# A gated delta-rule attention with a softplus MLP on one core: eight PSUM banks in one ring, and every item in a new order

## The chip, the core and the metric

The kernel runs on one core of a Trainium2 chip. The metric is the device time of one execution in microseconds (us), lower is better. The core has a matrix engine (PE; its weight loads are shown as PEld), VectorE (DVE), ScalarE (ACT), GpSimd (POOL) and SyncE (SP). Each works through its own list of instructions in order. DMAs are issued from the lists of SP, ACT and POOL and move data between memory (HBM) and SBUF. PE writes its results to PSUM, which is cut here into eight tiles of 128 x 512 floats, called banks in this text; DVE and ACT read them out.

## What is computed

Four batches and eight heads (32 in all), 768 time steps, head width 48. For each head a 48 x 48 state is carried through time:

```python
B, H, S, D = q.shape                       # 4, 8, 768, 48
k_n = k / (np.linalg.norm(k, axis=-1, keepdims=True) + 1e-06)
state = np.zeros((B, H, D, D)); y = np.zeros_like(q)
for t in range(S):
    readout = einsum('bhd,bhde->bhe', q[:, :, t], state)
    y[:, :, t] = g[:, :, t] * readout
    v_old = einsum('bhde,bhd->bhe', state, k_n[:, :, t])
    state += beta[:, :, t, None, None] * outer(k_n[:, :, t], v[:, :, t] - v_old)
```

The result, as 3072 tokens of 384 features, goes through a two-layer MLP, with `w_in` 384 x 2048 and `w_out` 2048 x 384:

```python
x = y.transpose(0, 2, 1, 3).reshape(3072, 384)
h = x @ w_in
out = softplus(h) @ w_out
```

## The kernel before

**Tiling.** Time is cut into 12 chunks of 64 steps. Within a chunk the recurrence is turned into small matrix products: the strictly triangular system that each chunk's keys make is inverted, and the state passes from chunk to chunk. Two batches sit side by side on the 128 partitions, so a 64-row product fills a quarter of PE and four of them run at a time. The chunks' systems are inverted in six pairs (`GROUPS`).

**Items.** The code first records the work as items (`Program.add`), each with the engines that may do it, what it depends on, and the buffers it uses. By name, in the order in which one chunk runs through them:

- `load` (L302, L305): q, k, v, g of a chunk, two DMAs of 192 KB each, from SP.
- `ksq`, `red`, `sqrt` or `pow`, `eps` (L351 to L383): the norm of k. `cast` or `kmul` (L209, L211, L406): q and k to fp16. `trs` (L422, L454): their transposes on PE. `kev`, `qev`: eviction of these from PSUM into `kqt`.
- `gram` (L516; for chunks 0 and 1 split into `gramk` and `gramq`, with `gramd`, L540, for the diagonal blocks): the products of keys with keys and queries. `kkc`, `kd`: evictions into `kk`, `dn`. `mask` (L498): the masked part into `mt`.
- `ln`, `pick`, `prep`, `step` (L597 to L671): the forward substitution of 16 x 16 blocks for a pair of chunks, 15 steps on DVE or POOL. `ca`, `cb` (L686, L688): the result as fp16 into `ta` and `tw`. `st` (L714): DVE transposes `ta` into `dn` and `tw` into `tb` and `td`. `tx`: a copy of half of `tb` to the other partitions.
- `xmm` (L744), `xs` (L753), `tmm` (L768), `td2`, `zmm` (L789), `z`: the inverse is put together from its blocks.
- The chain through the state: `ks` and `qs` (L826), `w` (L866), `umm` (L880), `u1`, `zu` (L893), `u2`, `smm` (L910), `s` (L924), `ymm` (L936), `y` (L950), `ytr` (L963), `xt`. Each hop is a product on PE and an eviction by DVE or ACT.
- The MLP: `g1` (L989), `soft` (L1001, the softplus on ACT), `g2` (L1016), `o` (eviction into `osb`), `store` (L1035). 96 `g1` and 96 `g2`; a `g2` is four of the 16 products that a sum in PSUM needs, so four `g2` share a bank. `wload` (L330) brings the weights, from POOL.
- `fill` (L1046): four products of the identity that nobody reads. 40 are recorded, and the order uses as many as it names.

Copies and evictions go through one helper, so all have the line L209 (on ACT), L211 or L213.

**Order.** Nothing is scheduled at run time. The string `_ORDER` names every item once with its engine letter (P, D, A, G for POOL, S), and `emit` issues them in that order: each engine gets its own items in the order of the string. A buffer is taken from its ring when the first item that uses it is emitted, and goes to the ring's end when the last one is. An item waits on the chip for what it depends on and for the last reader of the buffer's earlier content.

**PSUM.** The banks are three rings: five (`d`) for all products of the attention, two (`h`) for `g1` and fills, one (`o`) for the sums of `g2`:

```python
p_d = ring("d", 5, [P, 512], F32, psum)
p_h = ring("h", 2, [P, 512], F32, psum)
p_o = ring("o", 1, [P, 512], F32, psum)
```

**PE's two modes.** Products of 64 rows or fewer (gram, xmm, tmm, zmm, and the chain) use parts of the array, and transposes, g1, g2 and fills use all of it. The text calls a change from the one kind to the other in PE's list a border.

## Time and profile before

| | |
|---|---|
| runs | 242.34, 242.52, 244.88 us; median 242.52 |
| profiled execution, first to last instruction | 241.5 us |
| its own time beyond the span | not given; the median lies 1.0 us above the span |
| instructions | 11396, of them 5020 products on PE |
| data read / written by DMA | 25.26 MB / 4.72 MB, 124 GB/s over the span |
| first `g1` / last `g2` ends | 40.5 us / 237.6 us |

How to read the views that follow. The page's first part gives each engine's busy time, share of the span and number of instructions; a row of digits gives tenths in 40 equal slices, and PEclk the clock that PE was granted. In the timeline a row is start, duration, engine, line, operation, out<-in with sizes, a count, and in brackets how long the engine was idle before it and what ended that. PE's products are pipelined: a row's duration holds the time until the last one has drained, so the cost of a group is the distance from its start to the next group's start. The view by stage gives busy time and instructions of each engine between two moments.

### The profile page before, as it was taken

Reading aid. Unit: us, or ns where it says so; the run is one execution under the profiler, and the core shown is the slowest. Engines: PE = TensorE matmul, PEld = TensorE weight load, DVE = VectorE, ACT = ScalarE, POOL = GpSimd, SP = SyncE. Lnnn points to the kernel's source line nnn. Section 1 sums busy time; section 2 is a strip of 40 time slices with the busy share of each in tenths; the row PEclk is TensorE's granted clock in tenths of the full one; section 3 lists DMA queues with packets and bytes.
Section 4 is the critical chain, followed back from the end, with each engine's and each line's share of the span. In section 5 each row is a group of like instructions: output and inputs, shape, how many; then the busy total and the mean of one; then the engine's idle time right before and its main releaser. Section 6 shows DMA issues by size and latency. Waiting matters only on the chain.

```text
span 241.5 us, 11396 instructions
## 1 busy us (share of the span) xinstructions
PE 219.4 (91%) x5020; PEld 135.6 (56%) x5020; DVE 161.7 (67%) x368; ACT 152.8 (63%) x292; POOL 113.7 (47%) x197
## 2 busy tenths in 40 slices
PE   7645877879988999999999999999999999999983
PEld 2423455646764664556655566655565555677751
DVE  2768699888897889987899757896496310623000
ACT  5767576764982778876895767757363674143540
POOL 8740393875779778989597482016620000000000
PEclk9985599999999999999999999999999999999999
DMA  6999989999999399961889514962302311303112
GB/s 102 182 245 137 167 135 190 176 173 180 180 217 167 57 177 164 162 113 35 150 153 184 97 30 94 160 122 52 69 21 52 68 34 25 64 19 81 35 33 65
DMA packets 86833, 27.57 MB, mean 114 GB/s; under 512 B 77048, under 2 KB 86776, under 8 KB 86784
## 3 DMA queue, kind: packets, MB, share of 16 engines
q1 hardware_dynamic: 80624, 20.83, 52.6%
q0 software_dynamic: 3840, 3.17, 8.5%
q10 hardware_dynamic: 2320, 2.85, 5.2%
q8 instruction: 39, 0.64, 1.2%
q14 instruction: 10, 0.08, 0.1%
HBM read 25.26 MB, written 4.72 MB: 124 GB/s over the span
## 4 chain that ended last, share of the span: by engine, by line
PE 75%; DMA 7%; DVE 6%; SPq 4%; issue 3%; ACT 2%; POOL 1%; DVEq 0%; ACTq 0%; POOLq 0%
PE o L1016 27%; PE h L989 26%; DMA w_in<-in_moe_w_in_dram 4%; PE d L826 3%; SPq L305 3%; PE d L936 3%; PE d L516 2%; DMA f<-in_q_dram 2%; PE d L422 2%; PE d L963 2%; PE d L454 2%; PE d L880 2%; PE d L910 2%; PE d L893 2%; PE d L768 1%
## 5 line engine op out<-in xcount | busy, mean ns | idle before, releaser
L1016 PE MATMUL o<-w_out,ga 128*128 128x384 f16 x384 | 77.7, 327 | 0.7 <-ACT osb L209 0.6
L1001 ACT ACTIVATE ga<-h 128x512 f16<-128x512 f32 x96 | 56.5, 599 | 29.8 <-PE h L989 25.9
L989 PE MATMUL h<-xt,w_in 128*128 128x512 f16 (+1 forms) x384 | 74.0, 327 | 0.5 <-DMA w_in<-in_moe_w_in_dram 0.3
L989 PEld LDWEIGHTS <-w_in 128*128 128x128 f16 x384 | 34.5, 98 | 21.2 <-DMA w_in<-in_moe_w_in_dram 0.8
L1016 PEld LDWEIGHTS <-ga 128*128 128x128 f16 x384 | 33.7, 98 | 21.8 <-issue 0.8
L664 POOL TENSOR_TENSOR tmp<-nn,tt 128x78 f32<-128x78 f32 (+7 forms) x53 | 19.2, 362 | 16.1 <-DVE tt L671 13.0
L373 POOL TENSOR_TENSOR nv<-nv,half_c 128x16 f32<-128x16 f32 x8 | 23.5, 2940 | 6.6 <-DVE nv L362 6.5
L671 POOL TENSOR_TENSOR tt<-tt,tmp 128x78 f32<-128x78 f32 (+7 forms) x53 | 20.4, 385 | 4.2
L498 DVE TENSOR_TENSOR mt<-d,mask 128x256 f16<-128x256 f32 x48 | 18.2, 413 | 4.5 <-PE d L516 3.5
L209 ACT ACTIVATE kqt<-d 128x1024 f16<-128x1024 f16 (+1 forms) x18 | 18.0, 1000 | 4.8 <-PE d L454 3.6
L211 DVE CAST u<-d 128x384 f16<-128x384 f32 x20 | 10.9, 554 | 14.3 <-PE d L880 7.9
L209 ACT ACTIVATE u<-d 128x384 f16<-128x384 f32 x28 | 13.0, 490 | 11.8 <-PE d L880 5.4
L1046 PE MATMUL h<-ident 128*128 128x512 f16 x52 | 18.1, 493 | 1.7 <-DVE ident L197 1.7
L209 ACT ACTIVATE kk<-d 128x256 f16<-128x256 f32 x37 | 13.4, 386 | 6.3 <-PE d L516 5.4
L209 ACT ACTIVATE osb<-o 128x384 f32<-128x384 f32 x19 | 9.3, 492 | 9.4 <-PE o L1016 9.3
L454 PE MATMUL d<-ident,qn 128*128 128x128 f16 x96 | 8.5, 243 | 6.7 <-ACT qn L209 5.9
L950 DVE TENSOR_TENSOR yg<-d,f 128x384 f16<-128x384 f32 x24 | 12.3, 551 | 2.9 <-PE d L936 2.8
L924 DVE TENSOR_TENSOR s<-s,d 128x384 f16<-128x384 f16 x20 | 10.4, 542 | 5.7 <-PE d L910 4.3
L644 POOL TENSOR_TENSOR nn<-ln,beta_l 128x256 f32<-128x256 f16 x8 | 6.1, 780 | 14.2 <-DVE ln L627 14.2
L209 ACT ACTIVATE xt<-d 128x768 f16<-128x768 f16 x10 | 8.1, 813 | 7.0 <-PE d L963 7.0
L866 DVE TENSOR_TENSOR w<-f,d 128x384 f16<-128x384 f32 x22 | 11.3, 545 | 1.4 <-ACT xt L209 0.7
L362 DVE TENSOR_REDUCE nv<-f 128x16 f32<-128x768 f32 x12 | 11.3, 942 | 1.0 <-ACT f L351 1.0
(117 smaller groups left out, 346.7 us busy)
## 6 DMA issues: line engine op xcount, KB each, us to landing
f<-in_k_dram SPq DMA_DIRECT2D x24, 192.0 KB, 5.7
f<-in_q_dram SPq DMA_DIRECT2D x24, 192.0 KB, 5.6
f<-in_v_dram SPq DMA_DIRECT2D x24, 192.0 KB, 5.3
f<-in_g_dram SPq DMA_DIRECT2D x24, 192.0 KB, 5.3
out_dram<-osb ACTq DMA_DIRECT2D x29, 96.0 KB, 2.7
out_dram<-osb SPq DMA_DIRECT2D x19, 96.0 KB, 2.8
w_in<-in_moe_w_in_dram POOLq DMA_DIRECT2D x4, 384.0 KB, 7.9
w_out<-in_moe_w_out_dram POOLq DMA_DIRECT2D x4, 384.0 KB, 8.4
```

Of the source, the lines that this page charges most:

```text
L209: nc.scalar.activation(o, x, AF.Copy, scale=float(sign))
L362: lambda en: nc.vector.tensor_reduce(nvs().rearrange("p (a h) -> p a h", a=2), ksq.ap, mybir.AxisListType.X, ALU.add),
L373: nc.gpsimd.tensor_tensor(nvs(), nvs(), half_c[:, :NU], ALU.pow)
L454: nc.tensor.transpose(o[:, j], qn.ap[:, j].rearrange("p m d -> p (m d)"), ident)
L498: nc.vector.tensor_tensor(mt[c][m].ap[:, NP * p : NP * p + NP], gb[m].ap.rearrange("p (i b) -> p i b", i=NP)[:, :, n : n + C], mask[:, Non ...
L664: ENG[en].tensor_tensor(t, nn.ap[:, :, j : j + 1, j + 1 :].broadcast_to([P, 2, w, n]), tt.ap[:, :, :w, j : j + 1].broadcast_to([P, 2, w, n ...
L671: ENG[en].tensor_tensor(rows, rows, t, ALU.add)
L950: lambda en, m=m: nc.vector.tensor_tensor(heads(yg.ap, m), hd(yp[m].ap), heads(gf.ap, m), ALU.mult),
L989: nc.tensor.matmul(hp.ap[:, n * b : n * b + n], w_in[:, j, f * P : (f + 1) * P], xt.ap[:, j, t0 : t0 + n], start=(j == 0), stop=(j == 2),)
L1001: lambda en, hp=hp, o=gb: nc.scalar.activation(o.ap, hp.ap, AF.Softplus),
L1016: nc.tensor.matmul(op.ap[:, :DM], b.ap[:, col + c0 : col + c0 + 128], w_out[:, f, :], start=(f == 0), stop=(f == NF - 1),)
L1046: nc.tensor.matmul(hp.ap, ident, ident[:, None, :].broadcast_to([P, 4, P]))
```

## The change

Three edits. The eight banks become one ring that all products share. The items that need beta of the later chunks no longer hang on the norms: `setup[2]`, which the `eps` of chunks 2 and up wait for, loses the eight beta loads; `diag`, which reads beta, waits for them as before. And `_ORDER` is another permutation of the items, with other engines for some of them.

```diff
-    p_d = ring("d", 5, [P, 512], F32, psum)
-    p_h = ring("h", 2, [P, 512], F32, psum)
-    p_o = ring("o", 1, [P, 512], F32, psum)
+    p_d = p_h = p_o = ring("d", 8, [P, 512], F32, psum)
...
                 beta_it.append(add("bload", f"{r}{x}{a}", "S", bload))
-    setup[2] += beta_it
...
 _ORDER = """
-S26 S25 P138 P161 S33 S34 P151 A12 G4 S44 A173 S43 G2 A169 D176 P177 P174 D0 G227 A178 P188 D170 A15
+P138 P157 P133 S25 S26 S34 S33 G3 G8 G403 G201 G13 G10 G0 A169 D1 D4 D227 D12 D14 D173 D176 P177
...
```

What the strings hold, counted: 378 items on PE before and 373 after (13 fills and 8), 321 and 344 on DVE, 316 and 279 on ACT, 121 and 120 on POOL, 123 and 138 on SP. Of the 48 stores ACT issues 29 before and 14 after, SP the rest. Of the 90 substitution steps DVE does 32 before and 40 after. PE's list has 170 borders before and 142 after. The changed program's lines are lower by 2 or 3.

Three places. The first is ACT's list in the first pair of chunks. `tw` and `ta` are the results of the substitution, `kqt` is an eviction of transposed keys or queries, `qn` a cast, `td` the evictions that follow tmm, and `f` at L351 (L348 in the new program) the square of a chunk's k. Before:

```order
L351 ACTIVATE f_77<-f_79 128x768
L209 ACTIVATE qn_90<-f_83 128x2x8x48
L209 ACTIVATE kqt_103<-d_171 128x16x64
L686 ACTIVATE tw_119<-tt_117,mx 128x2x16x16 x2
L209 ACTIVATE tx_123<-tb_122 64x512
L209 ACTIVATE qn_91<-f_84 128x2x8x48
L209 ACTIVATE td_125<-d_170 128x8x2x16
```

After:

```order
L207 ACTIVATE kk_97<-d_175 128x4x64
L683 ACTIVATE ta_120<-tt_118,mx 128x16x16
L683 ACTIVATE tw_119<-tt_118,mx 128x2x16x16 x2
L207 ACTIVATE qn_91<-f_81 128x2x8x48
L348 ACTIVATE f_80<-f_83 128x768
L207 ACTIVATE td_125<-d_168 128x8x2x16
```

The cast and the eviction of a later q stood ahead of `tw` and are gone from there; a half of `ta` stands there now; and the square of chunk 2's k, which POOL did before (`f_75<-f_74` in the next excerpt), stands between `tw` and `td` on ACT.

The second is POOL's list up to the second weight load. `w` is the first chunk's right-hand side, `tt` and `tmp` belong to a substitution step, `tx` is the copy of `tb`. Before:

```order
L664 TENSOR_TENSOR tmp_115<-nn_113,tt_117 128x78
L671 TENSOR_TENSOR tt_117<-tt_117,tmp_115 128x2x3x13
L353 TENSOR_TENSOR f_75<-f_74 128x768
L211 COPY tx_123<-tb_122 64x512
L211 COPY kk_99<-pat 128x16x32
L330 DMA w_in<-in_moe_w_in_dram 128x3x512 x2
```

After:

```order
L855 TENSOR_TENSOR w_131<-f_80,nv_92 128x384
L209 COPY z_130<-pat 128x8x32
L209 COPY kk_99<-pat 128x16x32
L327 DMA w_in<-in_moe_w_in_dram 128x3x512
L209 CAST qn_90<-f_82 128x2x8x48
L661 TENSOR_TENSOR tmp_115<-nn_113,tt_118 128x56
L668 TENSOR_TENSOR tt_118<-tt_118,tmp_115 128x2x14x2
L350 TENSOR_TENSOR f_77<-f_84 128x768
L855 TENSOR_TENSOR w_132<-f_80,nv_92 128x384
L327 DMA w_in<-in_moe_w_in_dram 128x3x512
```

The first weight load has moved ahead of the substitution's step, which is now one of the last steps (128x56, two columns left) instead of an early one (128x78).

The third is PE's list where chunk 9's `umm` (L880, in the new program L877) ends. Before, a `g2` (L1016) follows:

```order
L880 LDWEIGHTS td_126
L880 MATMUL d_172<-w_131,td_126 64x48
L880 LDWEIGHTS td_126
L880 MATMUL d_170<-w_131,td_126 64x48
L1016 LDWEIGHTS ga_155
L1016 MATMUL o_175<-w_out,ga_155 128x384
```

After, the `qs` of the same chunk (L823):

```order
L877 LDWEIGHTS td_126
L877 MATMUL d_173<-w_133,td_126 64x48
L877 LDWEIGHTS td_126
L877 MATMUL d_172<-w_133,td_126 64x48
L823 LDWEIGHTS kqt_100
L823 MATMUL d_170<-s_144,kqt_100 64x48
```

There a border has gone: `umm`, `qs` and `zmm` of chunk 9 stand together, where each had stood between two `g2` or beside one other group.

More of the change, by code (lines that the diff above doesn't have):

```diff
@@ new lines @@
+P956 P958 A372 A373 A963 P966 A967 P968 P970 P951 D330 D331 D332 G381 D382 G333 D336 D334 D338 P389
+A337 A335 A377 A971 A957 P749 A969 D339 P343 D344 D345 D751 G383 G342 P952 P964 S81 S82 S53 S83 S84
+S48 S47 G449 A341 A959 A953 P346 A348 D384 A390 A347 G491 G469 P352 P972 P960 D340 D750 D354 P753
+D385 P979 P386 A961 A755 A754 P973 D353 D450 D470 P349 D351 A387 P396 P391 A965 A350 A397 A398 A393
+A392 D399 D400 D395 D394 P752 P756 A757 A476 A758 P974 P942 P975 P762 S114 S100 S54 S56 S75 D401
@@ new lines @@
+D402 D405 D763 D764 P759 D760 G451 D406 D452 A976 S977 S113 S55 S97 S76 S89 S98 S61 S62 P980 P355
+P765 P943 A766 A357 A356 D761 P767 D769 D768 P944 P358 D359 P771 A773 A360 D772 P770 P945 P774 P981
+D775 A776 P780 P477 P982 S92 G471 G407 G408 G409 G453 G410 G411 D412 G413 D472 D782 D781 P783 P454
+A946 A978 S69 S70 S90 A456 A478 G492 D414 D784 P777 P457 S99 P994 P1000 P1006 D455 D473 D779 D778
+A557 A983 A995 D558 P474 P998 S105 S64 S947 S91 P992 P986 S71 A1007 A1001 P1016 D475 A999 A987 G415
@@ new lines @@
+G416 G417 G418 G419 G420 G421 D458 P464 P785 G564 A423 A1017 P1002 P1004 A993 A466 A1005 A1003 D422
+D424 D425 D426 D427 D787 D468 D786 G537 G429 G579 D430 D467 P988 P996 P1010 P431 A989 A465 A997 D432
+D433 A1011 P990 P440 G580 G645 P434 P484 D428 S108 S72 S107 S955 S106 A991 D435 D486 D441 D442 D488
+P1008 A436 A1009 P1012 A1013 D538 S985 P1018 P789 P479 P459 P1019 A790 A485 A461 A791 A481 A480
+P1025 D462 D482 D460 D483 D487 D463 P1014 A1015 D489 D490 D493 G559 G632 G494 G495 D496 D497 G498
@@ new lines @@
+D512 D511 D1036 P1046 P1056 A1047 A1057 A546 P1068 P1066 A1069 P1054 D571 D646 D510 D515 D514 S101
+D570 S111 S109 A1067 A1055 D540 A568 P1052 P1048 A1053 A1049 G517 P1070 P821 P519 P572 D521 D520
+D822 P1072 P1050 A573 A1071 A518 A1073 P1074 P1062 D576 D575 D574 D823 G541 G667 G668 P522 A1051
+A523 D524 A1063 A1075 P528 D530 D516 P542 P1058 A1059 P1060 P1078 D543 P825 A1061 P525 P547 D529
+D626 G627 A527 D549 A827 S86 P1079 P1092 D526 D548 S103 S1038 S85 S1045 S88 S115 S87 D550 D826 P1076
+A1077 A954 P552 A553 D551 D555 A554 D556 D577 D578 D581 D582 P1080 P1093 G647 P824 P531 A532 S118
@@ new lines @@
+S1044 S116 P828 P1094 P1081 P1085 A829 A830 A533 D1082 P1099 P831 P834 D832 D833 P1086 P839 P1095
+D836 D841 D840 D835 A1096 S1098 G652 S1097 P1087 P534 P843 A845 A535 D536 D844 P842 P1100 P846 P1101
+P1088 A848 A847 S110 S1037 S93 P852 P849 P837 D628 D629 P1102 D853 D854 P855 P630 D850 D1103 D851
+P633 P653 A838 A1089 A856 P1106 A1107 A634 P1110 A1111 P1108 P1112 A1113 P1136 P1114 A1137 A1109
+D648 G583 G584 G585 G586 G587 G588 G589 G590 G591 G592 G593 D594 S95 D654 D631 D595 G649 P1128 P1116
@@ new lines @@
+A1117 P1122 A1123 A1129 P1134 A1115 S96 S1090 S1091 S120 S1105 D596 D597 D598 D600 D601 D602 D599
+D603 D604 P650 P607 P857 A651 A1135 D605 D609 D858 D608 D859 G606 P1130 P1124 A1131 A1125 P1118
+A1119 P610 P660 P616 P1132 D618 D664 D663 D611 P1120 P1138 P1126 S1083 D617 D612 D661 A662 A1133
+A1121 A1127 S117 S119 P861 P640 A863 A642 P613 D644 D615 D862 A641 D643 A614 P1139 P1145 P1140 P860
+P619 P864 A866 P1141 D865 P867 P870 P1146 A1142 D620 D621 D868 D869 P875 D872 D871 P635 P655 D659
+D877 D639 P1147 A657 D656 D637 D876 D658 D638 S1144 S1104 S1143 P1152 P1148 P1153 A1149 A636 A1150
@@ new lines @@
+D691 D692 G693 G694 P695 A1183 P893 D696 D697 A1151 D895 D894 P1220 P698 P1213 A1197 P1198 A699 A700
+P701 D702 P897 D899 D703 D898 P1206 P1199 P1214 P704 P896 D706 D705 P1207 P900 P1200 P1215 P1201
+A902 A901 P707 P906 D907 D908 P1208 P1221 P909 A1209 A1202 S1210 A910 P903 A1211 P1222 P1240 P1228
+D1216 D708 A1241 A1229 D905 D904 P911 D913 P1230 P1236 P1238 D1223 D912 S1224 A1218 A1231 A1237
+A1239 P1234 D709 P915 A917 D916 S1225 P914 P710 D711 P1226 P1232 A712 A1217 A1227 P918 D920 P1242
+P1249 A1233 D919 P921 P1243 A1235 S1203 S1204 D923 D922 P1250 P924 P1244 P1251 D925 P1260 P1256
@@ L1133 @@
+A1257 P1268 P1258 P1266 A1259 P1252 P1245 P1272 P1262 A1261 D1253 S1255 A1263 D1246 P1279 P1264
+A1265 A1267 S1254 S1248 S1247 P1273 P1270 P1280 A1271 P1274 P1281 A1269 P1275 P1282 A1276 A1278
+S1277 D1283 S1284 S1285
 """
```

89 lines of the change are left out of this document (24 added, 65 removed).

## Prediction

> **What bounds the kernel now.** I read the page's head and slices first, then busy time by stage, then the order of time on PE in a late and in the first stage.
>
> ```profile
> span 241.5 us, 11396 instructions
> PE 219.4 (91%) x5020; PEld 135.6 (56%) x5020; DVE 161.7 (67%) x368; ACT 152.8 (63%) x292; POOL 113.7 (47%) x197
> PEclk9985599999999999999999999999999999999999
> PE 75%; DMA 7%; DVE 6%; SPq 4%; issue 3%; ACT 2%; POOL 1%; DVEq 0%; ACTq 0%; POOLq 0%
> ```
>
> The fourth line is the chain that ended last: three quarters of it is PE. Where PE is full shows the view by stage (stage, its length, then busy time and instructions of PE, PEld, DVE, ACT, POOL; then granted clock, DMA share, GB/s):
>
> ```profile
> 0.00:26.00 26.00, 15.92 (x265) 8.90 (x266) 17.51 (x61) 17.00 (x34) 11.99 (x27) 0.82 1.02 166
> 26.00:40.50 14.50, 11.80 (x338) 6.34 (x336) 12.04 (x26) 10.29 (x20) 9.63 (x13) 0.85 1.07 161
> 40.50:84.00 43.50, 38.89 (x1100) 28.03 (x1100) 37.71 (x81) 28.69 (x58) 32.22 (x43) 1.00 1.05 167
> 84.00:237.60 153.60, 152.75 (x3342) 92.37 (x3328) 94.43 (x203) 96.34 (x181) 59.88 (x115) 1.00 0.49 88
> ```
>
> From 84 us to 237.6 us PE lacks 0.85 us of 153.6. There, only less PE time counts. Before 84 us PE has gaps, part of what it does is fill, and the DMA engines are full (shares above 1). So the change can win in three places: PE's own cost after 84 us, the start, and the end.
>
> **Part 1: borders between PE's two modes.** The change's order only permutes items, but PE pays when it passes from the 64-row products (gram, chain) to the full ones (g1, g2, transposes) and back. The timeline of PE shows the price (start, duration with drain, line; start to start is the cost):
>
> ```profile
> 175.54 0.82 PE L1016 MATMUL o<-w_out,ga 128*128 128x384 f16 x4
> 176.29 0.43 PE L789 MATMUL d<-td,kk 64*64 64x32 f16 x32
> 176.66 0.82 PE L1016 MATMUL o<-w_out,ga 128*128 128x384 f16 x4
> ...
> 177.78 0.83 PE L1016 MATMUL o<-w_out,ga 128*128 128x384 f16 x4
> 178.44 0.50 PE L963 MATMUL d<-ident,yg 128*128 128x128 f16 x6
> 178.87 0.43 PE L744 MATMUL d<-dn,kk 64*64 64x32 f16 x32
> 179.15 0.44 PE L826 MATMUL d<-s,kqt 48*64 48x48 f16 x32
> ```
>
> Four g2 products followed by a 64-row group take 176.29 - 175.54 = 0.75 us, followed by a full one 178.44 - 177.78 = 0.66. A 64-row group followed by full ones takes 176.66 - 176.29 = 0.37, followed by another such group 179.15 - 178.87 = 0.28. So each border costs 0.09 us. Counted in the two orders of PE from the first g1 on, the old one has 156 borders and the new one 122: 34 fewer, 34 x 0.09 = 3.1 us. Nothing hides it where PE is full. **-3.1 us.** Its ends are -2.5 (ten of them fall into waits) and -3.1. All other PE items are the same in number, except the fills.
>
> **Part 2: the start.** The first g1 begins at 40.51 us. In order of time, all engines (the row of 31.69 is a piece of the chain that ended last):
>
> ```profile
> 13.87 1.05 DVE L597 STREAM_TRANSPOSE ln<-dn 128x512 uint32<-128x512 uint32 x1 [0.89 <-ACT dn L209]
> 17.42 0.26 DVE L664 TENSOR_TENSOR tmp<-nn,tt 128x96 f32<-128x96 f32 x1 [0.92 <-POOL tt L671]
> 20.94 1.91 PE L1046 MATMUL h<-ident 128*128 128x512 f16 x4
> 24.34 0.21 DVE L671 TENSOR_TENSOR tt<-tt,tmp 128x30 f32<-128x30 f32 x1
> 25.41 1.07 DVE L714 STREAM_TRANSPOSE dn<-ta 128x512 uint32<-128x512 uint32 x1
> 25.96 1.02 ACT L209 ACTIVATE kqt<-d 128x1024 f16<-128x1024 f16 x1 [1.12 <-PE d L454]
> 26.88 1.32 ACT L686 ACTIVATE tw<-tt,mx 128x512 f16<-128x512 f32 x2
> 28.45 1.06 DVE L714 STREAM_TRANSPOSE tb<-tw 128x512 uint32<-128x512 uint32 x1
> 29.73 0.96 PE L744 MATMUL d<-dn,kk 64*64 64x32 f16 x64
> 30.41 0.76 DVE L753 TENSOR_TENSOR xs<-d,mk 128x256 f16<-128x256 f32 x2 [0.63 <-PE d L744]
> 30.87 1.62 POOL L330 DMA_DIRECT2D w_in<-in_moe_w_in_dram  x2
> 31.22 0.20 PE L768 MATMUL d<-tb,xs 64*64 64x32 f16 x2 [0.52 <-DVE xs L753]
> 31.69 8.77 DMA w_in<-in_moe_w_in_dram
> 32.04 1.03 PE L1046 MATMUL h<-ident 128*128 128x512 f16 x4
> 38.85 0.25 DVE L383 RECIPROCAL nv<-nv 128x16 f32<-128x16 f32 x1
> 40.51 1.49 PE L989 MATMUL h<-xt,w_in 128*128 128x256 f16 x12 [0.34 <-DMA w_in<-in_moe_w_in_dram]
> ```
>
> The substitution of the first pair of chunks ends at 24.55 (24.34 + 0.21); its product tmm (L768) starts at 31.22, so 6.67 us lie between. Two queues cause that. ACT evicts another chunk's q first and writes tw at 26.88, 2.3 us late, so DVE transposes tb at 28.45. And on PE a q transpose, two fills and a gram stand ahead of xmm (L744), whose input dn is there at 26.48 and which starts at 29.73. In the new order ACT goes straight to ta and tw, and PE's transpose of q4 stands behind tmm. Worked from the same rows: one ta on ACT as long as a tw (0.66), two tw (1.32), tb (1.06) with a mask of 0.4 ahead of it, xs (0.76), tx on DVE (0.3): 4.5 us in place of 6.67. The substitution itself ends about 0.9 us earlier: its transpose (13.87) waited 0.89 us for an eviction of dn, which ACT now does ahead of other work; the 0.92 us for POOL's turn at an early step (17.42) shrinks to DVE's own 0.5, and a turn of POOL at a late step costs as much again. So tmm comes at 24.55 - 0.9 + 4.5 = 28.1: -3.1 us.
>
> Behind that, two loads can be late. ACT now holds the square of chunk 2's k ahead of td2, and PE the transpose of q4 ahead of zu. The second half of k2 is the 21st load of 192 KB. With 384 KB of weights ahead of it, 4.4 MB at the 166 GB/s of the first stage end at about 28.5 us, and the square takes 0.84: td2 at 29.4, where the old distance (31.22 to the first td at 31.74) gave 28.6. q4 follows a load later, and its cast, transpose and the wait for them take about 0.5 us more. In return POOL issues the first w_in load ahead of the q2 cast, by 19 us instead of 30.87, so w_in no longer ends the wait at 40.51; and xt goes to DVE. Summed along the chain, the first g1 comes at 36.2.
>
> Against that stands the clock.
>
> ```profile
> 28.00:30.00 2.00, 2.00 (x24) 0.50 1.25 161
> 30.00:32.00 2.00, 1.48 (x100) 0.88 0.22 33
> L1046 PE MATMUL h<-ident 128*128 128x512 f16 x52 | 18.1, 493 | 1.7 <-DVE ident L197 1.7
> ```
>
> The granted clock was 0.50 in 28 to 30 us, full soon after, and four fills take 1.91 us at half and 1.03 at full clock. The old order has 13 fills (x52, four each), the new one 8, none behind xmm of chunk 1, so full clock may come back only with the dense work. I add 1.0 us: the 64-row groups of the chain and the first g1 at half clock, some 2 us of PE work of which half lies on the path. Ends: 0 and 3. First g1 at 37.2: **-3.3 us.** The Trainium skill ("TensorE: Matmul & The Clock Gate", Part 1) states that full clock returns after at least one busy window of about 3.4 us. By that rule the sparse chain would stay at half clock until a window of dense work is through; with 3.4 us at half speed my 1.0 would be 1.7 and the sum 0.7 us higher. The trace agrees in kind: full clock came behind the only stretch (26 to 30 us) that fills had closed.
>
> Ahead of that first g1, the new order has also done the transposes of k2 and k3 and one more gram, which the old one does behind it. Six transposes take 178.87 - 178.44 = 0.43 us with a border, so eight without one 0.45: two such and a gram of 0.2 make **-1.1 us.** They fall into PE's gaps.
>
> **Part 3: from there to 84 us.** The stage of 43.5 us has 38.89 busy, so 4.6 us of gaps, and two fills of 0.9 us each that the new order leaves out. They covered waits, and I cost them at nothing. Is there room to run earlier? DVE was busy 37.71 of 43.5 us, DMA at 1.05. So part of the lead is given back to loads and to DVE: **+1.5 us**. Ends: -1.8 (fills gone, no wait in their place) and +4.4 (the whole lead lost). I take a value in the middle, because the new order defers transposes of chunks 6 and 7, so it needs fewer loads by the same point.
>
> **Part 4: one ring of banks.** The end shows the one place where a bank is waited for on the path:
>
> ```profile
> 234.25 0.49 ACT L209 ACTIVATE osb<-o 128x384 f32<-128x384 f32 x1 [0.92 <-PE o L1016]
> 234.79 2.76 PE L1016 MATMUL o<-w_out,ga 128*128 128x384 f16 x16 [0.58 <-ACT osb L209]
> 237.59 0.49 ACT L209 ACTIVATE osb<-o 128x384 f32<-128x384 f32 x1 [2.85 <-PE o L1016]
> 238.10 0.47 SPq L1035 DMA_DIRECT2D out_dram<-osb  x1
> 238.11 0.50 ACTq L1035 DMA_DIRECT2D out_dram<-osb  x1
> ```
>
> The last g2 sums wait for the eviction of the only o bank: about 0.9 us of PE. With eight banks the two last sums interleave in two of them: -0.9. But three of the last four stores now stand on SP, at 0.5 us each, and the last ones behind one another: +0.5. **-0.4 us.** Elsewhere the ring is worth nothing, since PE does not wait after 84 us; in the new order at least 0.8 us of PE work lies between a bank's last product and its next.
>
> The beta wait that is dropped from the norms (L383) costs nothing either way: those ran at 38.85 with no idle time of DVE before them, so DVE's queue set their time and no load of beta. The 15 stores moved from ACT to SP leave SP's queue with waits behind which loads stand; after chunk 7 no load is short.
>
> **The sum.** -3.1 - 3.3 - 1.1 + 1.5 - 0.4 = -6.4 us on a span of 241.5, so 235.1. The three runs have a median of 242.52, 1.0 above the span; I keep that 1.0: **236.1**, told as 236.0.
>
> **The rivals.**
> - The lead is lost by 84 us: loads and DVE bind. For it speak the DMA share 1.05 and DVE's 37.71 of 43.5; against it the 5.8 us of DVE idle. Then -3.1 - 0.4 = -3.5: 239.0.
> - A load in front of a queue comes late: k2 ahead of td2 on ACT, or q4 ahead of zu on PE, by 5 us. For it: a w_in load took 8.77 us in that stage; against it: fewer weights compete there now. -6.4 + 5 = -1.4: 241.1, no change.
> - Slower, by the clock: full clock stays away while more than about 9 us of full-speed PE work passes (it then takes 9 us longer, against 6.4 won). From the first g1 on that means half clock until beyond 52 us. The time is 245. For it: fewer fills; against it: dense g1 products from 37 us on.
> - The order does not do what it says, and new waits appear where PE was full. If they eat what the borders save, the time is 236.1 + 3.1 = 239.2. Against it: between a product and the next one that needs its eviction, the shortest distance in PE work is 0.84 us in both orders behind 84 us.
>
> **How the numbers follow.** The forecast has 0.56, the lost lead 0.20, the late load 0.14, the clock and new waits 0.10. About 1% is what a measurement of this kernel can tell from no change: 240.1 to 244.9. Faster: 0.56 x 0.95 + 0.20 x 0.8 + 0.14 x 0.2 = 0.72. Slower takes the last 0.10 and a little more, 0.11, and 0.17 is left for the same. The range: all low ends give -3.1 - 4.3 (no clock loss) - 1.1 - 1.8 - 0.4 = -10.7, 231.8; upward it takes in the late load and a part of the slow case, 242.5.
>
> **What would show it.** Right: the first g1 near 37 us, tmm of chunk 0 near 28, PE within 1 us of full from about 80 us to its end, and no wait of PE on osb. Wrong: the first g1 at 40 or later with ACT waiting on k; half clock beyond 42 us; PE gaps behind 84 us, with DVE named; a stretch from 84 us on no shorter than the borders say.

## The result and the profile after

The new order is slower: 250.51 us (median of 4 runs, 249.46 to 253.76) against 242.51 (4 runs, 242.34 to 244.88), a ratio of 1.029 with a 95% interval of 1.022 to 1.037. The forecast was 236.0. Ratios leave out executions more than 1.5% above the fastest of their kernel (here 253.76 us), and because the profiles of the runs "new start, old rest" and "fills" below are of such executions, the table gives no stages for them. The profiled execution took 249.46 us, with a span of 247.7 (before: 241.5).

The page of the new kernel, its head, its clock slices and its chain:

```profile
span 247.7 us, 11372 instructions
PE 219.0 (88%) x5000; PEld 140.1 (57%) x5000; DVE 182.7 (74%) x399; ACT 134.7 (54%) x270; POOL 117.0 (47%) x188
PEclk9975755997979999999999999999999999999999
PE 23%; DVE 3%; POOL 2%; issue 1%; ACT 0%; POOLq 0%; DVEq 0%
```

PE is as busy as before (219.0 and 219.4 us) although the new order has five fills and 34 borders less, so it does its work at a worse price: part of it ran at half clock. DVE has 21.0 us more. The clock shows a second stretch of 5 and two single dips where the old kernel is at 9 from 31 us on. The chain was followed back through 29% of the span only, so I read by stages instead (the stages start at 0, 26 us, the first g1 and 84 us, and end with PE's last product; columns as before):

```profile
0.00:26.00 26.00, 17.30 (x308) 8.77 (x308) 21.79 (x63) 14.44 (x29) 14.35 (x31) 0.80 1.08 172
26.00:43.59 17.59, 11.92 (x317) 9.13 (x316) 13.67 (x28) 10.55 (x20) 10.49 (x12) 0.61 1.17 168
43.59:84.00 40.41, 35.13 (x907) 25.52 (x907) 34.07 (x70) 25.25 (x53) 31.84 (x40) 0.92 0.93 137
84.00:243.42 159.42, 154.65 (x3472) 96.72 (x3472) 112.65 (x240) 84.47 (x169) 60.28 (x107) 1.00 0.48 89
```

The first g1 begins at 43.59 us, not at 37.2 (before: 40.51). Behind 84 us PE lacks 159.42 - 154.65 = 4.77 us, where the old kernel lacks 0.85. So the time is lost twice: ahead of the first g1 (3.1 us), and behind it. From the first g1 to PE's last end the new kernel takes 243.42 - 43.59 = 199.8 us, the old one 237.55 - 40.51 = 197.0, although the new order has fewer borders and more work already done. In that stretch PE's busy time fell from 191.6 to 189.8 us, in spite of 6.8 us at half clock that the old kernel does not have there; its idle time rose from 5.4 to 10.1.

**Where the start went.** Steps of DVE's first substitution (all L661 and L668), the first of them begun ahead of POOL's work and seven stretched, and POOL beside them, in the timeline (start, duration, engine, line):

```profile
16.37 0.26 DVE L668 TENSOR_TENSOR tt<-tt,tmp 128x96 f32<-128x96 f32 x1
16.50 0.83 POOL L855 TENSOR_TENSOR w<-f,nv 128x384 f16<-128x384 f32 x1 [3.43 <-DMA f<-in_v_dram]
16.69 0.78 DVE L661 TENSOR_TENSOR tmp<-nn,tt 128x110 f32<-128x110 f32 x1
17.28 0.44 POOL L209 COPY z<-pat 128x256 f16<-128x256 f16 x1
17.50 0.35 DVE L668 TENSOR_TENSOR tt<-tt,tmp 128x110 f32<-128x110 f32 x1
17.67 0.65 POOL L209 COPY kk<-pat 128x512 f16<-128x512 f16 x1
17.88 0.57 DVE L661 TENSOR_TENSOR tmp<-nn,tt 128x120 f32<-128x120 f32 x1
18.27 0.83 POOL L327 DMA_DIRECT2D w_in<-in_moe_w_in_dram  x1
18.49 0.82 DVE L668 TENSOR_TENSOR tt<-tt,tmp 128x120 f32<-128x120 f32 x1
19.10 0.89 POOL L209 CAST qn<-f 128x768 f16<-128x768 f32 x1
19.35 0.79 DVE L661 TENSOR_TENSOR tmp<-nn,tt 128x126 f32<-128x126 f32 x1
...
24.91 1.47 POOL L350 TENSOR_TENSOR f<-f 128x768 f32<-128x768 f32 x1
24.99 1.45 DVE L661 TENSOR_TENSOR tmp<-nn,tt 128x30 f32<-128x30 f32 x1 [0.18 <-POOL tt L668]
26.33 0.84 POOL L855 TENSOR_TENSOR w<-f,nv 128x384 f16<-128x384 f32 x1
26.48 0.76 DVE L668 TENSOR_TENSOR tt<-tt,tmp 128x30 f32<-128x30 f32 x1
```

Each of the seven ends 0.1 to 0.2 us behind the POOL instruction beside it, however long that is; a step of this size takes 0.2 to 0.3 us alone. The excess is 0.5 + 0.1 + 0.3 + 0.5 + 0.5 + 1.2 + 0.6 = 3.7 us. In the old kernel POOL did nothing from 17.4 to 26.9 us. The Trainium skill ("SBUF — State Buffer", section "SBUF: two separate sides") states that DVE with two inputs in SBUF and a POOL instruction that reads SBUF lock one port pair against each other for a whole instruction; the rows of POOL's six operations on data agree.

**Where the rest went.** Of the 4.77 us that PE lacks behind 84 us, 2.6 are three waits for a late result: a copy of tb on POOL (chunk 4), an xt on ACT (chunk 7) and an xs on DVE (chunk 8).

```profile
105.69 0.20 PE L765 MATMUL d<-tx,xs 64*64 64x32 f16 x2 [0.94 <-POOL tx L209]
...
161.94 0.81 PE L986 MATMUL d<-xt,w_in 128*128 128x512 f16 x3 [0.76 <-ACT xt L207]
...
172.60 0.20 PE L765 MATMUL d<-tb,xs 64*64 64x32 f16 x2 [0.91 <-DVE xs L750]
```

Another 1.3 us are waits for a bank. The plainest case: gram of chunk 9 writes its first two banks at 125.64, and the next gram needs one of them.

```profile
125.64 0.42 PE L513 MATMUL d<-kqt 48*64 48x128 f16 x16
...
134.67 0.37 DVE L495 TENSOR_TENSOR mt<-d,mask 128x256 f16<-128x256 f32 x1
...
135.08 0.38 ACT L207 ACTIVATE kk<-d 128x256 f16<-128x256 f32 x1 [1.58 <-DVE mt L495]
135.36 1.08 ACT L998 ACTIVATE ga<-d 128x512 f16<-128x512 f32 x2
...
135.51 0.21 PE L513 MATMUL d<-kqt 48*64 48x128 f16 x1 [0.25 <-ACT kk L207]
136.00 0.41 PE L513 MATMUL d<-kqt 48*64 48x128 f16 x14 [0.28 <-ACT ga L998]
```

The mask of the first bank stands in DVE's list behind the end of a substitution, so it runs at 134.67. The kk eviction of the same bank waits for it on ACT, and two softplus evictions (135.36) wait behind that one. So the bank is held from 126.05 to 135.46, 9.4 us, and PE stops for both banks of the second gram, 0.25 + 0.28 us. In each of these places PE waits for an item that stands late in another engine's list.

### The profile page after: what moved, and what is told of

Read it like the earlier page. It is cut to its first block, busy times and chain, and to the rows that moved or that the text cites. A ratio compares the mean times of both kernels' runs of the same rounds, so it can differ in the third digit from the quotient of the medians.

```text
span 247.7 us, 11372 instructions
## 1 busy us (share of the span) xinstructions
PE 219.0 (88%) x5000; PEld 140.1 (57%) x5000; DVE 182.7 (74%) x399; ACT 134.7 (54%) x270; POOL 117.0 (47%) x188
## 3 DMA queue, kind: packets, MB, share of 16 engines
q10 hardware_dynamic: 1120, 1.38, 2.4%
## 5 line engine op out<-in xcount | busy, mean ns | idle before, releaser
L1013 PE MATMUL d<-w_out,ga 128*128 128x384 f16 x384 | 73.2, 329 | 0.5 <-DVE osb L209 0.3
L986 PE MATMUL d<-xt,w_in 128*128 128x512 f16 (+1 forms) x384 | 69.5, 331 | 2.5 <-ACT xt L207 0.8
L998 ACT ACTIVATE ga<-d 128x512 f16<-128x512 f32 x96 | 53.2, 600 | 25.0 <-PE d L986 23.7
L661 POOL TENSOR_TENSOR tmp<-nn,tt 128x56 f32<-128x56 f32 (+7 forms) x45 | 17.4, 387 | 19.9 <-DVE tt L668 17.5
L661 DVE TENSOR_TENSOR tmp<-nn,tt 128x78 f32<-128x78 f32 (+7 forms) x39 | 15.7, 402 | 6.1 <-POOL tt L668 4.1
L668 POOL TENSOR_TENSOR tt<-tt,tmp 128x56 f32<-128x56 f32 (+7 forms) x45 | 16.8, 373 | 3.5
L1043 PE MATMUL d<-ident 128*128 128x512 f16 x32 | 12.7, 555 | 2.4 <-DVE ident L195 1.7
L209 DVE COPY osb<-d 128x384 f32<-128x384 f32 x11 | 6.1, 553 | 11.4 <-PE d L1013 11.4
L668 DVE TENSOR_TENSOR tt<-tt,tmp 128x78 f32<-128x78 f32 (+7 forms) x39 | 12.5, 320 | 1.3
L863 DVE TENSOR_TENSOR w<-f,d 128x384 f16<-128x384 f32 x22 | 11.6, 545 | 2.4 <-PE d L823 1.3
L513 PE MATMUL d<-kqt 48*64 48x128 f16 (+1 forms) x448 | 11.1, 222 | 1.8 <-ACT kqt L207 0.9
L403 POOL TENSOR_TENSOR kn<-f,nv 128x768 f16<-128x768 f32 x7 | 10.4, 1480 | 4.6 <-DVE nv L380 3.8
```

What stands on the lines that cost most here:

```text
L513: nc.tensor.matmul(gb[m].ap.rearrange("p (i b) -> p i b", i=NP)[HALF[r], i, lo:hi], x[:, :C], x[:, lo:hi],)
L661: ENG[en].tensor_tensor(t, nn.ap[:, :, j : j + 1, j + 1 :].broadcast_to([P, 2, w, n]), tt.ap[:, :, :w, j : j + 1].broadcast_to([P, 2, w, n ...
L668: ENG[en].tensor_tensor(rows, rows, t, ALU.add)
L863: lambda en, m=m: nc.vector.tensor_tensor(w1[m].ap, heads(vf.ap, m), hd(wp[m].ap), ALU.subtract),
L986: nc.tensor.matmul(hp.ap[:, n * b : n * b + n], w_in[:, j, f * P : (f + 1) * P], xt.ap[:, j, t0 : t0 + n], start=(j == 0), stop=(j == 2),)
L998: lambda en, hp=hp, o=gb: nc.scalar.activation(o.ap, hp.ap, AF.Softplus),
```

## Experiments

Sixteen runs, in this table with the place of the first g1 and the length from there to PE's last end. "Ratio" is against the kernel before, run in turn on the same chip (its medians there: 242.5 to 243.6 us).

| run | median us | ratio (95%) | first g1 | to PE's end |
|---|---|---|---|---|
| before | 242.51 | 1 | 40.51 | 197.0 |
| after | 250.51 | 1.029 (1.022 to 1.037) | 43.59 | 199.8 |
| old order, one ring | 241.75 | 0.992 (0.988 to 0.996) | 39.88 | 196.7 |
| new start, old rest | 249.87 | 1.023 (1.017 to 1.030) | - | - |
| old start, new rest | 251.59 | 1.032 (1.026 to 1.038) | 41.30 | 204.1 |
| quiet | 246.73 | 1.013 (1.004 to 1.022) | 39.78 | 199.6 |
| fills | 253.25 | 1.039 (1.032 to 1.046) | - | - |
| quiet, fills | 248.33 | 1.019 (1.015 to 1.024) | 40.38 | 202.1 |
| old order less fills | 245.90 | 1.011 (1.007 to 1.015) | 39.34 | 201.5 |
| old engines | 278.16 | 1.146 (1.139 to 1.153) | 44.49 | 226.6 |
| quiet, all substitutions | 246.80 | 1.019 (1.015 to 1.024) | 42.07 | 199.8 |
| borders alone | 262.65 | 1.085 (1.079 to 1.090) | 38.75 | 216.3 |
| quiet new to 92 us, then old | 252.85 | 1.043 (1.035 to 1.051) | 42.22 | 207.0 |
| old to 92 us, then new | 247.83 | 1.024 (1.014 to 1.033) | 39.25 | 202.8 |
| evictions forward | 247.08 | 1.020 (1.012 to 1.028) | 44.69 | 196.7 |
| all mended | 248.80 | 1.026 (1.019 to 1.033) | 39.56 | 202.3 |
| quiet, evictions forward | 243.69 | 1.007 (1.002 to 1.011) | 39.31 | 197.9 |
| the same, late substitutions | 244.00 | 1.005 (1.001 to 1.010) | 38.72 | 198.8 |

In the diffs below, items stand by name; "old" and "new" are the two orders.

### Is it the ring or the order?

```diff
 p_d = p_h = p_o = ring("d", 8, [P, 512], F32, psum)
-_ORDER = new
+_ORDER = old
```

> The old order word for word, on the new kernel's one ring of eight banks and without the beta load as a wait of the norms. If the loss of 8 us comes from the order (my theory), this runs as the kernel before, 242.5 within 1 us, with PE lacking less than 1.5 us from 84 us on. If the shared ring or the dropped wait costs something of itself (rival: a product waits for the bank of another kind, a load of beta now in the way), it lies above 244, with PE waits behind the evictions of o or h that the old kernel does not have.

It is the order. With one ring the old order is 0.8% faster than with three. PE lacks 0.29 us of 152.54 behind 84 us, and PE's wait of 0.58 us for osb ahead of the last sum is gone: the last 24 products take 4.28 us (237.55 - 232.53 = 5.02 before).

```profile
232.27 4.28 PE L1013 MATMUL d<-w_out,ga 128*128 128x384 f16 x24
```

The ring and the dropped beta wait were not told apart. This is the fastest kernel of the study.

### Crossing the orders at the first g1

```diff
-_ORDER = new
+_ORDER = new[:208] + old without these          (new start, old rest)
+_ORDER = old[:203] + new without these          (old start, new rest)
```

> The new order up to the first g1, and from there the old order for all items that are left. If the loss is made in the start (first g1 at 43.6 instead of 40.5, with 1.1 us of work done ahead of it), this takes some 2 us more than the kernel before, 244.5, and the rest of the loss must be in what follows. If the whole loss of 8 us comes from the start (the later loads and the clock drag on), it takes 249 or more. If only what follows loses, it stays within 1 us of 242.5.

> The old order up to the first g1, and from there the new order for all items that are left: the other half of the exchange. If the new waits behind 84 us and the ones between 44 and 84 us are the larger part of the loss (my theory: about 6 us of waits less 2.7 us of saved borders, and 2 to 3 us ahead of 84), this takes 247 to 249. If the start alone loses, it takes 239 to 242, since the borders and the end are still saved.

Both lost, the second more than either of its expectations had it, but neither tells the parts apart: fills that only the other order names came along and piled up right at the seam, five too many in the first and two in the second, at about 0.9 us each. The crossings were made again further back, without such fills.

### POOL beside the first substitution

```diff
 POOL
-w0 0.0, fixed z and kk, wload w0.2, cast q2, step 0.13, ksq 4, w0 0.1
+wload w0.2, ksq 4, w0 0.0, w0 0.1, fixed z and kk      (emitted behind step 0.14)
 DVE
-step 0.12, step 0.14
+step 0.12, step 0.13, step 0.14
 ACT
+cast q2
```

> The new order with POOL kept quiet during the first substitution: step 13 and the cast of q2 go to DVE and ACT, and two w0 products, the square of k4 and two fixed copies move behind step 14 on POOL. In the trace of the new kernel eight of DVE's steps last as long as the POOL operation beside them (0.78, 0.57, 0.82, 0.79, 1.45, 0.76 instead of 0.2 to 0.3 us), 3.7 us in all. If POOL's operations stretch them (theory: the two engines take turns at SBUF), the steps are all 0.2 to 0.3 long here, tmm of chunk 0 starts near 28.3 instead of 32.0 and the first g1 near 40; the time is up to 3.7 us less, 246.8. If something else stretches them (the DMA writing into SBUF, the clock), they stay as long, and the time stays at 250.

The first theory's numbers came: tmm of chunk 0 begins at 27.41, the first g1 at 39.78, 3.8 us earlier than in the new kernel, with a median of 246.73 (ratio 1.013 against 1.029). The same steps in this run's timeline:

```profile
17.17 0.28 DVE L661 TENSOR_TENSOR tmp<-nn,tt 128x120 f32<-128x120 f32 x1
...
23.30 0.21 DVE L668 TENSOR_TENSOR tt<-tt,tmp 128x30 f32<-128x30 f32 x1
...
24.00 1.47 POOL L350 TENSOR_TENSOR f<-f 128x768 f32<-128x768 f32 x1 [10.31 <-DMA f<-in_k_dram]
```

What kept POOL quiet here is the load of k4, for which its square waited until 24.00. The length behind the first g1 did not change (199.6 us): the start is one loss, and the rest is another.

### The clock

```diff
 PE (new order; the second run has the quiet start too)
+fill x3  ahead of xmm 0              (second run: x1)
+fill     behind tmm 0, ahead of zu 0 (second run: without zu 0)
+fill     ahead of ymm 0, behind smm 0, ahead of zu 1, ahead of ks 2
```

> The new order with nine fills more on PE, where it waits: three ahead of xmm of chunk 0, one each behind its tmm, ahead of its zu and its ymm and behind its smm, one ahead of zu of chunk 1 and one ahead of ks of chunk 2. Nothing else moves. In the trace of the new kernel half clock stood for 13.7 us from 29.2 on, behind a window of 3.4 us in which PE was busy to 0.16, and again for 3.4 us at 56.5 and at 70.2, behind windows of 0.60 and 0.57. If the clock is a cause (theory), it is full from about 26 us on, PE work that took 7.0 us too long behind 30 us takes its usual time, and the kernel runs 3 to 6 us shorter: 244.5 to 247.5. If half clock only fell on work that was waiting anyway (rival), the time stays at 250, or rises by up to 3 us for the fills in the way.

> Both at once: POOL quiet during the first substitution as in the run before, with the POOL copy of tx ahead of a weight load and two fixed copies (PE waited 2.0 us for it there), and six fills more. If port and clock are two causes that add up, this gives the 3.8 us of the quiet run, up to 2 us for tx and 3 to 5 us for the clock: 237 to 241, below the kernel before. If the clock is no cause, 245 to 248.

```diff
 PE (old order, one ring)
-fill x2 ahead of xmm 0, fill ahead of zmm 0, ymm 0 and g1 0
```

> The old order on one ring of banks, less five fills (two ahead of xmm of chunk 0, one each ahead of its zmm, ymm and first g1): the suspected cost put into the good kernel. If fills only cover waits and keep the clock (theory), half clock stays beyond 31 us until dense work is through, near 42 to 45 us, and the time is 3 to 5 us above the same order with its fills: 245 to 247. If fills stand in the way and the clock costs nothing (rival), it takes 240 to 242.

Fills taken out of the old order cost 4.1 us (245.90 against 241.75), as the clock theory said. Fills put into the new order won nothing: the medians are 2.7 and 1.6 us above those without them, and both times the intervals overlap. They did act on the clock: with them the quiet run spends 6.8 us at half clock behind 26 us, without them 17.1. So the theory holds for an order built around its fills, and fails as a remedy. Windows of the new kernel (bounds, length, busy time of PE, PEld, DVE, ACT and POOL, then the granted clock, DMA's share and GB/s):

```profile
25.82:29.24 3.42, 0.56 (x7) 0.17 (x6) 3.29 (x6) 1.91 (x4) 2.14 (x3) 1.00 1.28 181
29.24:32.65 3.41, 3.39 (x100) 1.85 (x99) 3.35 (x7) 1.51 (x3) 2.00 (x3) 0.50 1.37 195
32.65:36.06 3.41, 2.04 (x70) 1.72 (x71) 2.94 (x7) 2.32 (x7) 2.16 (x3) 0.50 1.00 127
...
42.89:46.30 3.41, 2.97 (x80) 2.16 (x78) 3.24 (x10) 2.59 (x4) 3.05 (x2) 1.00 1.20 196
```

The stretched steps leave PE empty from 26 us on (0.56 us of 3.42), and half clock follows for 13.65 us. In the quiet run, whose steps are not stretched, it still stands for 10.24 us from 28.63 on, so at most one window of 3.4 us comes with the stretched steps. The old order without the five fills stays at half until a dense window has passed:

```profile
28.32:31.74 3.42, 1.94 (x68) 1.67 (x72) 3.42 (x7) 2.64 (x5) 2.74 (x4) 0.50 0.69 75
...
41.98:45.39 3.41, 3.41 (x39) 2.84 (x41) 0.97 (x2) 1.19 (x2) 1.97 (x2) 0.50 1.26 185
45.39:48.80 3.41, 3.29 (x107) 2.41 (x100) 3.17 (x10) 2.64 (x8) 1.03 (x1) 1.00 1.24 165
```

### New rows, old engines

```diff
-every item behind ks 3 on its new engine
+111 of them on the engine of the old order, stores apart, at the same place
```

> The new order, with every item behind 85 us (from ks of chunk 3 on, stores apart) on the engine that the old kernel has for it: 111 items change engine, no item changes its place. From 84 to 204 us the new kernel's PE has 4.8 us of waits, the old one's 0.2. If they come from the new shares of the engines (DVE has 21 us more, and its steps stretch beside POOL), they fall below 2 us, and the time is 3 us less, 247.5. If they come from the order of the rows itself, they stay or grow: 250 or more.

The order fell apart, at 278.16 us with 25.8 us of PE idle behind 84 us. It shows only that rows and engines were chosen together; whether DVE's 21 us are too many cannot be read from it.

### The later substitutions

```diff
 POOL
-cast q9, ksq 8, tx 4.0        +tx 4.0, cast q9, ksq 8
-cast q8, kmul 9               +step 6.7, 6.8, 6.10   (cast q8 to ACT, kmul 9 to DVE)
-kmul 11 ahead of step 8.13    +kmul 11 behind step 8.14
 DVE
-qev 11, kev 10 ahead of step 8.12    +behind st 8.c
-w 8.0, xs 8.0                        +xs 8.0, w 8.0
 POOL, the start of the quiet run
-fixed z and kk, wload w0.0, tx 0.0   +tx 0.0, wload w0.0, fixed z and kk
```

> The quiet start as before (with tx ahead of a weight load and two copies on POOL, no fills added), and the same care for the substitutions of chunks 4, 6 and 8: POOL's cast of q9 and its square of k8 go behind its tx of chunk 4; the product k9 goes from POOL to DVE, the cast of q8 to ACT, and steps 7, 8 and 10 of chunk 6 to POOL; the product k11 goes behind step 14 of chunk 8, and two of DVE's evictions and one w product behind its last steps and masks. In the quiet run's trace the PE waits from 84 to 204 us are 4.4 us, 3.5 of them at xmm or tmm of chunks 4, 6 and 8, and steps there last as long as the POOL operation beside them (0.88, 1.45, 1.51 us). If late substitutions make these waits (theory), they fall to 1.5 us or less, tx of chunk 0 no longer holds tmm for 2.0 us, and the time is 3 to 4.5 us under the quiet run: 242 to 244. If DVE and PE simply have no slack in this order (rival), the waits appear behind other producers and the time stays above 245.

The rival was right. The waits at tx 4.0 and xs 8 went, and as many came behind ACT's evictions; the length from the first g1 on stayed at 199.8. And the start was 2.3 us later than in the quiet run. Its timeline shows why:

```profile
24.21 1.46 POOL L350 TENSOR_TENSOR f<-f 128x768 f32<-128x768 f32 x1 [10.15 <-DMA f<-in_k_dram]
24.36 1.38 DVE L661 TENSOR_TENSOR tmp<-nn,tt 128x30 f32<-128x30 f32 x1
```

The substitution ran 1.3 us later in this execution, and k4 landed ahead of its last step, so the square met it after all. An order that only happens to keep two engines apart doesn't keep them apart: there has to be something that POOL waits for.

### Borders alone

```diff
 PE (old order, one ring), first of 216 places that differ
-g2 1.1.0, trsq 7, zu 3, g2 1.1.4, ymm 3, smm 3, g2 1.1.8, ytr 3, gram 6.0
+trsq 7, g2 1.1.0, zu 3, g2 1.1.4, ymm 3, smm 3, gram 6.0, g2 1.1.8, ytr 3
```

> The old order on one ring of banks with nothing moved but PE's own items, and those only behind ks of chunk 3 and by a few places: PE passes 136 times between 64-row and full products instead of 170, 34 times less, as many as the new order saves. All other engines have the old order. If a border costs 0.09 us where PE is full (the price of the prediction), PE ends 3.1 us earlier, and the time is 238.7 beside 241.75 for the same ring with the old PE order. If the saving goes into waits, since products stand closer to what they wait for (rival), it stays at 241 to 243, with PE waits behind 84 us.

The rival by far: 262.65 us. Behind 84 us PE has 154.93 us of work in a stage of 171.10:

```profile
84.00:255.10 171.10, 154.93 (x3288) 94.34 (x3276) 92.74 (x200) 93.18 (x178) 59.07 (x112) 0.99 0.45 76
```

Moving PE's items by a few places (13 at most) and nothing else brought 16 us of waits. In 8.0 of them PE stands for a bank and starts within 0.13 us of its last reading; the others end with a late result of another engine. The other engines' lists are in order too, so an eviction that comes a product later can hold up all that stands behind it there. That this is the cause is argued: the ring gives a bank to whichever item is emitted first, so the move deals the banks anew as well, and the run does not tell the two apart.

### Crossing at 92 us

```diff
-_ORDER = new
+_ORDER = quiet[:488] + old without these
+_ORDER = old[:492] + new without these
```

> The new order with the quiet start up to 92 us (488 items; the two orders have done the same PE work there but for one g2 group), and from there the old order for all that is left, with no fill of the old start carried over. In the quiet run's trace PE has at 84 us done as much useful work as the old order on one ring (44.2 and 43.8 us). If the loss that is left is made behind that point (theory), this runs within 1.5 us of the old order on one ring, 240.5 to 243.5, with under 1 us of PE waits from 100 us on. If the new start leaves the other engines behind, so that the loss comes later whatever the order (rival), it takes 245 or more.

> The other half: the old order up to 92 us (492 items), then the new order. If the new rows behind 92 us lose by themselves (theory), PE has 3 to 5 us of waits from 100 to 204 us in spite of an undisturbed start, pays 32 borders less, and the time is 243.5 to 246, above 241.75 of the old order on one ring. If those waits only followed from the late start and the half clock (rival), they fall under 1 us, the borders are saved, and the time is 238 to 240.5, the best of all.

Both took longer than their theories had it. The first has a fault of its own at the seam: the order of the loads there makes ACT wait for q of chunk 9, and PE with it for 6 us.

```profile
100.96 0.84 ACT L207 ACTIVATE qn<-f 128x768 f16<-128x768 f32 x1 [6.44 <-DMA f<-in_q_dram]
...
102.23 1.01 PE L986 MATMUL d<-xt,w_in 128*128 128x512 f16 x2 [6.01 <-ACT osb L207]
```

Behind that, from 104 us on, its old rows leave PE 0.27 us idle in 145.30. The new rows behind the old start, with a clock of 1.00 and the first g1 at 39.25, leave PE idle for 3.1 us between 84 and 104 us, around their own seam, and for 3.94 us behind it:

```profile
104.00:242.00 138.00, 134.06 (x2982) 84.32 (x2979) 93.63 (x201) 69.89 (x141) 43.71 (x74) 1.00 0.35 70
```

So the new rows wait by themselves, whatever came ahead of them, and the old rows don't.

### Banks held behind the substitutions

Which bank an item gets follows from the order, so each wait of PE can be set beside the end of the last instruction that had read the bank before. From 40 us on, in the new kernel PE stands idle ahead of 14 items that then start within 0.13 us of that end, for 5.0 us in all (1.3 of them behind 84 us); in the old kernel ahead of 7, for 2.7 us (0.6 behind 84 us); on one ring in the old order ahead of 4, for 0.7 us (none behind 84 us). Seven evictions that hold banks, or that hold up the late xt, were moved:

```diff
 ACT
-cb 2.0, kkc 4.10, soft 1.14           +soft 1.6, kkc 4.10 (ahead of cb 2.1)
-eps 8 (DVE), kkc 9.00, soft 4.3       +kkc 9.01, kkc 9.00 (ahead of soft 4.9)
-o 4.1, xt 7                           +xt 7, o 4.1
 DVE
-st 4.c, w 4.1, mask 6.11, w 4.0, tx 4.1, mask 6.10
+st 4.c, mask 6.10, mask 6.11, w 4.1, w 4.0, tx 4.1
-cb 6.1 ... mask 9.01 ... st 6.a, mask 9.00
+mask 9.00, mask 9.01, cb 6.1 ... st 6.a
```

> The new order with seven evictions moved within their own engine's queue, no engine changed, PE's order untouched: on ACT the kk eviction of gram 4 goes ahead of the substitution's last evictions, that of gram 9 behind its twin, and one output eviction that waits for a store goes behind xt of chunk 7; on DVE two masks of chunk 6 go ahead of two w products and two masks of chunk 9 ahead of the substitution's end. In the trace of the new kernel PE waits 1.55 and 0.47 us at ks and xmm of chunk 2, 0.32 at tmm of chunk 4, 1.05 at gram of chunk 9 and 0.92 at g1 of chunk 6 for banks or queues that these free. If banks held too long are a cause (theory), those waits fall to under 1 us in all and the time falls by 2.5 to 4 us, to 246.5 to 248. If the engines are simply too full and the wait only moves (rival), it stays within 1 us of 250.5.

The median came as the theory had it, 247.08. By the ratios that is 0.9% of the time, and the two intervals overlap, so the time alone does not show the gain. The traces, one of each, do: 196.7 us behind the first g1, where the new kernel takes 199.8, and 3.60 us of PE idle behind 84 us in place of 4.77. Its own first g1 came 1.1 us later. Gram of chunk 9 no longer waits:

```profile
127.67 0.65 ACT L207 ACTIVATE kk<-d 128x256 f16<-128x256 f32 x2
128.08 0.76 DVE L495 TENSOR_TENSOR mt<-d,mask 128x256 f16<-128x256 f32 x2 [0.79 <-ACT kk L207]
...
134.37 0.40 PE L513 MATMUL d<-kqt 48*64 48x128 f16 x16
```

### Both causes mended

```diff
 POOL (new order), behind the quiet run's changes
-step 0.14 on DVE, ksq 4 on POOL       +step 0.14 on POOL, ksq 4 on ACT behind tw
+w0 0.0, w0 0.1, tx 0.0, wload w0.0, fixed z and kk    (behind step 0.14)
 ACT, DVE
+the seven evictions moved forward                     (third run: only this)
+the later substitutions as above                      (first two runs)
 POOL, DVE (first run only)
-ksq 5, step 2.14, red 5     +step 2.14, ksq 5 ... st 2.c, red 5
```

> All mended at once on the new order: POOL quiet beside the first substitution (the square of k4 on ACT, step 14 on POOL as a barrier ahead of the w0 products, tx ahead of a load and two copies), POOL's products, squares and casts moved from beside the substitutions of chunks 2, 4, 6 and 8, and the seven evictions moved forward. If port, banks and stores are the causes, the gains add: 3.8 to 5 us at the start, 2.5 to 4 from the evictions, 1 to 2 from the late substitutions: 239.5 to 243, level with the old order on one ring or below it. If the order has no slack anyway (rival), it stays above 245.

> The same, and POOL's work moved from beside the substitutions of chunks 4, 6 and 8, as in the run with all mended, but without its move of the square of k5, which there held tmm of chunk 2 for 3.8 us. If the late substitutions cost something of their own, this is 1 to 2 us under the run with the two causes alone, 241.5 to 242.5. If not, the two are equal within 1 us.

> The new order with the quiet first substitution (step 14 on POOL as a barrier, the square of k4 on ACT) and the seven evictions moved forward, nothing else. The quiet start alone gave 3.8 us, the evictions alone 3.4. If they are two causes that add (theory), this takes 250.5 - 3.8 - 3.4 = 243.3, within 1 us, level with the kernel before. If one stands in for the other (rival: the time won at the start is waited away at the same later places), it takes 246 to 247.

The first missed for a move that was my mistake. With the square of k5 later, POOL's power of its norm came to stand ahead of the second tx of chunk 2:

```profile
66.58 2.94 POOL L370 TENSOR_TENSOR nv<-nv,half_c 128x16 f32<-128x16 f32 x1 [3.50 <-DVE nv L359]
...
70.59 0.18 PE L765 MATMUL d<-tx,xs 64*64 64x32 f16 x1 [3.18 <-POOL tx L209]
```

Without that move the two causes give 243.69, a ratio of 1.007 in place of 1.029: 2.2 of the 2.9 per cent, about 5.4 us. Alone they gave 1.6% and 0.9%, so they add within the intervals, though the quiet start has another form here (a step on POOL as a barrier, the square on ACT). The 2.2% are clear of the intervals; the share of the evictions by itself is not. The later substitutions change nothing beside them (1.005 and 1.007). What is left against the old order on one ring is 1.5%. In that run PE still lacks 3.73 us behind 84 us, and the mean clock of the stage ahead is 0.92:

```profile
39.30:84.00 44.70, 39.52 (x1085) 28.33 (x1084) 37.65 (x77) 27.38 (x58) 35.40 (x48) 0.92 1.05 157
84.00:237.16 153.16, 149.43 (x3302) 93.47 (x3294) 109.46 (x232) 82.46 (x164) 56.72 (x100) 1.00 0.48 88
```

Which of its waits could still be taken out, and at what price in others, was not tried.

## Why the prediction was wrong

Between the forecast -6.4 us and the measured change of the span, 247.73 - 241.46 = +6.3, lie 12.7 us: 6.4 ahead of the first g1, and 6.4 between there and PE's last product (forecast -3.1 - 1.1 + 1.5 - 0.9 = -3.6, measured +2.8).

**The start, forecast -3.3 us, was +3.1.** The step that failed is "the substitution itself ends about 0.9 us earlier". It took the durations of DVE's steps from a trace in which POOL was idle beside them, and the new order puts six POOL operations and a weight load's issue next to them. The substitution began 1.0 us earlier (14.80, before 15.81), as read, but ended at 27.23 in place of 23.65. That cost 3.7 us, and the quiet run gave 3.8 back. I had counted POOL's turns in the substitution, which became fewer, and not what POOL does in the time that this frees.

The order of the evictions behind the substitution was read rightly, but for tx, of which one half is on POOL. In the quiet run tmm begins 27.41 - 23.51 = 3.9 us behind the last step (4.5 forecast, 6.67 before), and its products that need that half wait until 29.44. With quiet start and evictions forward tmm comes 27.93 - 23.64 = 4.3 us behind the last step, at 27.93, where 28.1 was forecast.

From there to the first g1 the forecast had 37.2 - 28.1 = 9.1 us. With both causes mended it is 39.31 - 27.93 = 11.4, and in the new kernel 43.59 - 32.03 = 11.6. Here the sentence on the transposes done ahead failed, "They fall into PE's gaps". In the run with quiet start and evictions forward:

```profile
35.64 1.06 PE L419 MATMUL d<-ident,kn 128*128 128x128 f16 x8
36.49 0.85 PE L960 MATMUL d<-ident,yg 128*128 128x128 f16 x6
...
37.99 0.86 PE L419 MATMUL d<-ident,kn 128*128 128x128 f16 x8
```

The transposes of later keys (L419) stand on the path. The transpose of the result (L960) starts 0.64 us behind its input, and the first g1 (39.31) 1.38 us behind xt, of which PE is idle for 0.46; in the old kernel these distances are 0.06 and 0.36. Half clock stood there for 6.8 us (10.2 in the quiet run), where the forecast had +1.0 for it, with ends 0 and 3; how much of the 2.3 us is its share is open.

**The clock, forecast +1.0 with a rival of 245 us.** Fewer fills did mean a longer half clock, as that rival had it, 13.65 us in one stretch from 29.2 us on and two dips of 3.4. (The prediction's rows of 1.91 and 1.03 us are one fill of four products each.) The argument against it, dense g1 products from 37 us on, failed with the start. That rival had half clock until beyond 52 us; here it ended at 42.9 and came back for the two dips. The price in an order that relies on its fills is 4.1 us; for the new order it stays open, since fills that shortened the half clock there did not shorten the time.

**Borders, forecast -3.1 us.** 34 borders went, and the price holds in the traces: behind 84 us a `g2` group that a full product follows takes 0.65 us from start to start (the median of 28 in the old kernel, of 19 in the new one), one that a 64-row group follows 0.74 (18 in each). But the sum was taken as a gain that stands by itself, because PE was full. PE's idle time behind 84 us rose from 0.8 to 4.8 us, more than the borders save. The run with 34 borders less and no other item moved took 20.9 us more than the same order with them. What makes PE full is that every eviction is done in time, and that is a property of the whole order, not of the stage.

**One ring, forecast "worth nothing" elsewhere.** This is the second step that failed: "at least 0.8 us of PE work lies between a bank's last product and its next". That distance was counted in PE's work, but the bank is free when its eviction has run, and that one stands in a list: for gram of chunk 9 it took 9.4 us. The rival "new waits appear where PE was full" was the right one, but it was argued away with that same distance, and priced only at what the borders save. The ring by itself is not the cause: the old order on one ring stands for only 0.7 us for such banks. Nor are the banks all of it: behind 84 us they are 1.3 of the 4.77 us, and the larger part, 2.6, are late results of the other engines. For those the forecast gave 0.84 us as the shortest distance between a product and the next one that needs its eviction, and this distance too was counted in PE's work.

**The end, forecast -0.4 us, was right.** Its -0.9 was read beside a row in which ACT, not PE, waits for 0.92 us (the one at 234.25); the old order on one ring saves 5.02 - 4.28 = 0.74 there. In the new kernel the last products run without a wait for osb:

```profile
240.01 3.41 PE L1013 MATMUL d<-w_out,ga 128*128 128x384 f16 x20
```

From PE's end to the end of the span it took 247.73 - 243.42 = 4.3 us, before 241.46 - 237.55 = 3.9, so the end costs 0.4 there (0.5 was forecast for the stores on SP). That the beta wait costs nothing is not contradicted by the old order on one ring.
